# Cached attention, decode step: value tiles loaded through ScalarE's DMA queue

## The chip, the cores and the metric

One Trainium2 chip, one core of it. The metric is device microseconds of one execution. A core has TensorE (PE: matmuls, with PEld for the loads of their weights), VectorE (DVE), ScalarE (ACT), GpSimd (POOL) and SyncE (SP). Each engine works through its own list of instructions in order. DMAs are issued by instructions in such a list; here SyncE and ScalarE issue them, each into a queue of its own, and 16 DMA engines move the bytes of both.

## What is computed

A decode step for 4 sequences of one token: adaptive layer norm, attention over a cache of 4096 keys and values for each of 32 heads of 128, then a gated MLP. Cut to what matters:

```python
h = _layernorm(x) * (1 + ca) + sa                    # 4 x 512
q = (h @ wq).reshape(B, 1, 32, 128)
scores = einsum('bhqd,bhkd->bhqk', q, k_cache) * 128 ** -0.5
o = einsum('bhqk,bhkd->bhqd', softmax(scores), v_cache)
x = x + ga * (o.reshape(B, 1, 4096) @ wo)
h = _layernorm(x) * (1 + cb) + sb
x = x + gb * gated_mlp(h, w_in, w_sp, b_sp, w_out)
```

The keys and the values are 134 MB each, in bf16, and each is read once. All other inputs together are some 14 MB.

## The kernel before, in words

The 32 heads x 4 sequences are cut into 32 steps `i` of one sequence and four heads (`NT` = 32, `L` = 31 the last). A step has one K tile and one V tile, each 128 partitions x 128 rows x 128 (4 MB, 32 KB in each partition). There are two buffers of K tiles (named `kt`) and two of V tiles (`vt`); the last V tile uses a `kt` buffer. K2 and V2 stand for the tiles of step 2 in what follows.

The order of the work is written out by hand, in the loop at L533. For step `i` it holds, in this order:

- `mult(i, 0)` and `mult(i, 1)` (L291, VectorE): the two halves of the K tile are multiplied by the query, in place. They need K of step `i` to have landed.
- `reduce_d(i, 0)` and `reduce_d(i, 1)` (L297, TensorE): 16 matmuls with the identity that add up parts of each product; `sum8` (L306, VectorE) adds the rest.
- `scores(i-1)` (L311 to L332): the maximum on VectorE, then four Exps on ScalarE (L329) that write the weights `pbd`.
- `load_k(i + 2)` (L557): K of two steps on, into the buffer that step `i` frees; it waits for the last matmul of `reduce_d(i, 1)`.
- `pv(i-2)` (L369, TensorE): 32 matmuls of the weights with V of step `i-2`.
- `load_v(i)` (L570; `load_v(1)` at L568 in step 0): V of step `i`, into the buffer that `pv(i-2)` has just read.
- `o_pick(i-3)`, `o_cols`, `o_scale`, `project`: the output of an earlier step, picked out of PSUM and multiplied by `wo`.

So the loads go out as K0, K1, V0 ahead of the loop, then K2, V1 in step 0, K3 in step 1, K4 and V2 in step 2, and K and V in turn from there. All of them, and those of the weights, are issued by SyncE in this order. SyncE starts with `wq` (L92) and `wm` (L95). In step 2, behind V2, it loads `wo_sb` in four parts (L584) and `wo_last` (L589). ScalarE issues four small loads: `c_sb` and `x_sb` at the start (L86, L88) and two single numbers into `sp_t` in step 2 (L572, L573).

In step 30 come V30, then V31 in five pieces (32, 32, 32, 16 and 16 rows a partition, `TAIL`), the MLP's weights `win_sb` (L602, two parts) and `wout_sb` (L604), and the last part of `w_mod` (L608, into a `vt` buffer). Behind the loop runs the end of the kernel: `pv(30)`, the 128 matmuls of `o_last` with V31 (L396), the projection, the second layer norm, the MLP (L694, L719) and the output.

Each DMA counts up one of eight semaphores when it lands. They are dealt out in turn, so that a DMA may have to wait for an earlier one that used the same semaphore.

Of the kernel before, what the change touches and what calls it, by code (L numbers as in the profile page):

```python
# [16 lines left out]
KC = 64  # L17
RD = 8
TAIL = (32, 32, 32, 16, 16)
# [8 lines left out]
def kernel(  # L28
# [16 lines left out]
    nc = tc.nc  # L45
# [8 lines left out]
    NJ = SK * HQ // P  # L54
# [8 lines left out]
    L = NT - 1  # L63
# [33 lines left out]
    def kv_view(cache, i):  # L97
        g, b = divmod(i, B)
        v = cache[b, g * HQ:(g + 1) * HQ].rearrange("h s d -> (h s) d")
        return v.rearrange("(p n) d -> p n d", p=P)  # L100

    kts, vts = {}, {}

    def load(dst, src, cuts):
        n0 = 0
        for n in cuts:
            nc.sync.dma_start(out=dst[:, n0:n0 + n, :], in_=src[:, n0:n0 + n, :])
            n0 += n

    def load_k(i):  # L110
        if i < NT:
            kts[i] = kvp.tile([P, NJ, DH], BF16, name="kt", bufs=2)
            load(kts[i], kv_view(A_k_cache, i), (KC, NJ - KC) if i == L else (NJ,))

    def load_v(i):

        vts[i] = kvp.tile([P, NJ, DH], BF16, name="kt" if i == L else "vt", bufs=2)
        load(vts[i], kv_view(A_v_cache, i), TAIL if i == L else (NJ,))

    load_k(0)  # L120
    load_k(1)
    load_v(0)

    ident_bf = consts.tile([P, P], BF16, name="ident_bf")
# [21 lines left out]
        out=sel32, in_=ident_f.rearrange("p (q r) -> p r q", r=R), axis=AX.X, op=ALU.add  # L146
# [10 lines left out]
    for g in range(G):  # L157
        nc.vector.tensor_reduce(out=selg[:, g:g + 1], in_=idr[:, g], axis=AX.XY, op=ALU.add)
    nc.vector.tensor_reduce(
        out=sel4, in_=ident_f.rearrange("p (c b) -> p b c", b=B), axis=AX.X, op=ALU.add  # L160
# [3 lines left out]
        out=mask8, in_=ident_f.rearrange("p (h u) -> p h u", h=2 * HQ), axis=AX.X, op=ALU.add  # L164
# [42 lines left out]
    def normed(pool, src, name, then=None, last=None):  # L207
# [24 lines left out]
        out=sg, in0=cx, scalar1=-60.0, scalar2=-1.0, op0=ALU.max, op1=ALU.mult  # L232
# [6 lines left out]
    def mod_cols(s0, n, dst):  # L239
# [20 lines left out]
        out=hs, in0=modA[:, DJ:2 * DJ, :], scalar=1.0, in1=xn, op0=ALU.add, op1=ALU.mult  # L260
# [174 lines left out]
    for n in set(SETS):  # L435
        picks[n] = consts.tile([P, n, P], BF16, name=f"pick{n}")
        for a in range(n):
            u = P // n
            nc.vector.tensor_copy(
                out=picks[n][:, :, a * u:(a + 1) * u],  # L440
                in_=ident_bf.rearrange("p (u r) -> p r u", r=n),
# [91 lines left out]
    for i in range(NT):  # L533
# [21 lines left out]
        sum8(i, 0)  # L555
        reduce_d(i, 1)
        load_k(i + 2)  # L557
        if i >= 1:
            norm_a(i - 1)
# [7 lines left out]
        if i == 0:  # L567
            load_v(1)  # L568
        elif 2 <= i < L:
            load_v(i)  # L570
        if i == 2:
# [11 lines left out]
            for n in SETS:  # L583
                nc.sync.dma_start(  # L584
                    out=wo_sb[:, h0:h0 + n, :],
                    in_=A_wo[h0 * DH:(h0 + n) * DH].rearrange("(p r) n -> p r n", p=P),
# [48 lines left out]
    def sums():  # L635
# [20 lines left out]
        out=x1m, in0=x1[:, :, :, None].to_broadcast([P, DJ, B, HQ]),  # L656
# [5 lines left out]
        out=nv2, in0=mq2[:, 0:1], scalar=mq2[:, 0:1], in1=mq2[:, 1:2],  # L662
# [7 lines left out]
        out=hl, in0=xs, scalar=mq2[:, 0:1], in1=cbT[:, :, BL], op0=ALU.subtract, op1=ALU.mult  # L670
    )
    nc.vector.scalar_tensor_tensor(
        out=hT2[:, :, BL], in0=hl, scalar=rsl, in1=sbT[:, :, BL], op0=ALU.mult, op1=ALU.add
# [13 lines left out]
    def gate(h, part):  # L687
# [24 lines left out]
        out=zz.rearrange("p f g b -> p g b f"), in0=z1[:, None].to_broadcast([P, 2, B, NH]),  # L712
# [11 lines left out]
    for k in range(DJ):  # L724
# [7 lines left out]
        out=mq3, in_=ps3.rearrange("p (g b f) -> p g b f", g=2, b=B), axis=AX.X, op=ALU.add  # L732
# [4 lines left out]
        out=rs3, in0=mq3[:, 1], scalar=LN_EPS, in1=rs3, op0=ALU.add, op1=ALU.subtract  # L737
# [3 lines left out]
        out=g8[:, 0, :], in0=mq3[:, 0, :], scalar=-1.0, in1=g8[:, 1, :], op0=ALU.mult, op1=ALU.mult  # L741
# [5 lines left out]
        out=t3[:, 2], in0=yb[:, 0], scalar1=spf[:, 1:2], scalar2=None, op0=ALU.mult  # L747
    )
    nc.vector.tensor_tensor(
        out=g8, in0=g8, in1=rs3[:, None, :].to_broadcast([P, 2, B]), op=ALU.mult  # L750
    )
    nc.vector.tensor_tensor(
        out=t3[:, 0:2], in0=g8[:, :, :, None].to_broadcast([P, 2, B, DJ]), in1=yb, op=ALU.mult
# [3 lines left out]
        out=tt, in_=t3.rearrange("p g b j -> p b j g"), axis=AX.X, op=ALU.add  # L757
# [37 lines left out]
```

## Time and profile before

| | us |
|---|---|
| median of 3 runs | 667.61 (667.01 to 668.0) |
| the profiled execution | 667.16 |
| its span, first to last instruction | 665.4 |
| around the span | 1.76 |

| engine | busy us | share of the span | instructions |
|---|---|---|---|
| PE | 400.9 | 60% | 2674 |
| PEld | 175.3 | 26% | 2674 |
| DVE | 419.5 | 63% | 589 |
| ACT | 85.2 | 13% | 278 |
| POOL | 3.8 | 1% | 17 |

All traffic together is 283.15 MB at a mean of 426 GB/s. A K tile lands 23.0 us after its issue, a V tile 30.6 us (medians).

How to read what follows: times in a row of the trace count from the start of the span. A row of the order of time has start, duration, engine, line, operation, output and input, and in brackets the idle time of the engine ahead of it with what ended that. The rows of VectorE at L291 that end with a wait for a K tile show when that tile landed. A digit of the slices is the busy share of a fortieth of the span (16.6 us) in tenths. DMA share is the mean busy share of the 16 DMA engines; in short windows it can exceed 1. Rows marked SPq and ACTq are issues of DMAs by SyncE and ScalarE.

### The profile page before, as it was taken

How to read it: one execution, taken by the hardware profiler on the slowest of the kernel's cores; microseconds unless marked ns; L12 is line 12 of the kernel's file. 1: busy time of each engine (PE TensorE's matmuls, PEld its weight loads, DVE VectorE, ACT ScalarE, POOL GpSimd, SP SyncE). 2: the span in 40 equal slices, each digit the busy share in tenths (PEclk: the TensorE clock that was granted, in tenths of full speed). 3: DMA queues.
4: the chain of work that ended last, by engine and by line, in shares of the span. 5: the costliest groups of instructions: out<-in, count | busy, mean ns of one | idle time of the engine just before them, and what ended most of it. 6: DMA issues, size and time to landing. Idle time of an engine off the chain costs nothing.

```text
span 665.4 us, 6511 instructions
## 1 busy us (share of the span) xinstructions
PE 400.9 (60%) x2674; PEld 175.3 (26%) x2674; DVE 419.5 (63%) x589; ACT 85.2 (13%) x278; POOL 3.8 (1%) x17
## 2 busy tenths in 40 slices
PE   1195795556456647555665567566555467677676
PEld 0132331222122213222222223222222222232235
DVE  3485592776556776665577656657765666776833
ACT  1021120111011111101111110111110011111112
POOL 1000000000000000000000000000000000000000
PEclk9998987777898788889877778787767986887975
DMA  8999999999999999999999999999999999999996
GB/s 363 450 425 431 431 411 439 438 426 428 441 434 424 432 439 433 423 437 436 427 429 438 436 424 432 438 436 425 429 440 435 427 427 440 433 428 424 446 412 250
DMA packets 13537, 283.15 MB, mean 426 GB/s; under 512 B 1340, under 2 KB 3268, under 8 KB 4420
## 3 DMA queue, kind: packets, MB, share of 16 engines
q1 hardware_dynamic: 13488, 282.73, 99.0%
q8 instruction: 21, 0.34, 0.2%
q14 instruction: 8, 0.07, 0.0%
q10 hardware_dynamic: 20, 0.01, 0.0%
HBM read 282.73 MB, written 0.00 MB: 425 GB/s over the span
## 4 chain that ended last, share of the span: by engine, by line
DMA 57%; DVE 28%; PE 13%; issue 1%; SPq 0%; DVEq 0%
DMA kt<-in_A_k_cache_dram 51%; DVE kt L291 21%; PE red L297 12%; DMA vt<-in_A_v_cache_dram 3%; DMA wout_sb<-in_B_w_out_dram 3%; DVE osb L381 2%; DVE S L306 1%; DVE mrow L315 1%; DVE osb L377 1%; PE ops L369 1%; DVE mt L319 1%; DVE nM L321 0%; PE qps L277 0%; DVE mb L317 0%; DVE nM L322 0%
## 5 line engine op out<-in xcount | busy, mean ns | idle before, releaser
L297 PE MATMUL red<-kt,ident_bf 128*128 128x512 bf16 x1024 | 301.4, 460 | 235.0 <-DVE kt L291 235.0
L291 DVE TENSOR_TENSOR kt<-kt,qbc 128x8192 bf16<-128x8192 bf16 x64 | 282.8, 4420 | 185.3 <-DMA kt<-in_A_k_cache_dram 184.3
L297 PEld LDWEIGHTS <-ident_bf 128*128 128x128 bf16 x1024 | 118.5, 116 | 410.9 <-issue 283.8
L329 ACT ACTIVATE pbd<-S,nM 32x128 bf16<-32x128 f32 x128 | 74.0, 578 | 505.2 <-DVE nM L322 463.4
L369 PE MATMUL ops<-vt,pbd 128*16 128x512 bf16 x992 | 63.8, 393 | 1.3 <-DMA vt<-in_A_v_cache_dram 1.3
L306 DVE TENSOR_REDUCE S<-red 128x64 f32<-128x512 f32 x64 | 43.7, 684 | 5.9 <-PE red L297 5.9
L381 DVE SCALAR_TENSOR_TENSOR osb<-ops,selg,osb 128x128 f32<-128x128 f32 x93 | 32.6, 351 | 3.3
L329 ACT ACTIVATION_READ_ACCUMULATOR pbd<-S,nM 32x1 f32 x128 | 32.1, 251 | 0.0
L369 PEld LDWEIGHTS <-pbd 128*16 128x16 bf16 x992 | 23.4, 90 | 31.3 <-issue 9.5
L389 PEld LDWEIGHTS sm<-sel,osb 128*128 128x128 f32 x62 | 11.6, 194 | 8.0 <-issue 2.2
L377 DVE TENSOR_SCALAR osb<-ops,selg 128x128 f32<-128x128 f32 x31 | 10.1, 325 | 5.2 <-PE ops L369 5.2
L389 PE MATMUL sm<-sel,osb 128*128 128x4 f32 x62 | 9.3, 220 | 2.4 <-DVE osb L381 2.3
L281 ACT CAST qbc<-qps 128x512 bf16<-128x512 f32 x8 | 4.7, 587 | 45.4 <-PE qps L277 45.4
L277 PE MATMUL qps<-wq_sb,hTb 128*32 128x512 bf16 x128 | 9.2, 412 | 1.6 <-DVE hTb L265 0.9
L315 DVE TENSOR_REDUCE mrow<-S 128x1 f32<-128x128 f32 x32 | 9.2, 286 | 1.1
L245 PE MATMUL sm<-cT,wm_sb 128*128 128x4 bf16 x80 | 3.0, 173 | 8.2 <-DMA wm_sb<-in_w_mod_dram 8.2
L319 DVE STREAM_TRANSPOSE mt<-mb 128x32 f32<-128x32 f32 x32 | 6.8, 212 | 1.1
L340 DVE TENSOR_SCALAR rsb<-mask,rs 128x4 f32<-128x4 f32 x32 | 7.2, 224 | 0.4 <-ACT pbd L329 0.4
L321 DVE TENSOR_REDUCE nM<-mt 128x1 f32<-128x32 f32 x32 | 6.0, 186 | 1.1
L317 DVE COPY mb<-mrow 128x32 f32<-128x32 f32 x32 | 5.8, 181 | 1.1
L494 PE MATMUL sm<-wo_sb,od 128*4 128x512 bf16 x24 | 5.7, 379 | 0.0
L322 DVE TENSOR_SCALAR nM<-nM 128x1 f32<-128x1 f32 x32 | 4.9, 153 | 1.1
(136 smaller groups left out, 89.0 us busy)
## 6 DMA issues: line engine op xcount, KB each, us to landing
kt<-in_A_k_cache_dram SPq DMA_DIRECT2D x31, 4096.0 KB, 23.0
vt<-in_A_v_cache_dram SPq DMA_DIRECT2D x31, 4096.0 KB, 30.6
wq_sb<-in_A_wq_dram SPq DMA_DIRECT2D x1, 4096.0 KB, 12.2
kt<-in_A_k_cache_dram SPq DMA_DIRECT2D x2, 2048.0 KB, 16.5
wo_sb<-in_A_wo_dram SPq DMA_DIRECT2D x3, 1024.0 KB, 22.9
kt<-in_A_v_cache_dram SPq DMA_DIRECT2D x3, 1024.0 KB, 25.5
wm_sb<-in_w_mod_dram SPq DMA_DIRECT2D x1, 2560.0 KB
win_sb<-in_B_w_in_dram SPq DMA_DIRECT2D x2, 896.0 KB, 24.2
```

The lines of the kernel that those rows point to most:

```text
L277: nc.tensor.matmul(qp[R * q:R * (q + 1)], lhsT=hTb[:, k, b, :], rhs=wq_v[:, k, gs, q, :], start=(k == 0), stop=(k == DJ - 1), tile_positio ...
L291: nc.vector.tensor_tensor(out=kt, in0=kt, in1=bc(qbc[:, g, b, :], KC), op=ALU.mult)
L297: nc.tensor.matmul(red, lhsT=ident_bf, rhs=kt[:, :, m * RD:(m + 1) * RD], start=(m == 0), stop=(m == DH // RD - 1),)
L306: nc.vector.tensor_reduce(out=st[i, "S"][:, kc * KC:(kc + 1) * KC], in_=st.pop((i, "red", kc)), axis=AX.X, op=ALU.add,)
L315: nc.vector.tensor_reduce(out=mrow, in_=S, axis=AX.X, op=ALU.max)
L319: nc.vector.transpose(mt, mb)
L329: nc.scalar.activation(out=pbd[r, :, q], in_=S[r, :], func=AF.Exp, bias=nM[r, :], scale=att_scale, accum_out=rs[r, :],)
L340: nc.vector.tensor_scalar(out=st[g, "rsb"][:, b, :], in0=mask4, scalar1=st.pop((i, "rs")), scalar2=None, op0=ALU.mult)
L369: nc.tensor.matmul(opss[i % 2][g:g + G * HQ], lhsT=pbds[i % 3][:, n, :], rhs=vts[i][:, n, :], start=(m < 4), stop=(m >= NJ // G - 4), tile ...
L377: nc.vector.tensor_scalar(out=osb, in0=ops[:, 0, :], scalar1=selg[:, 0:1], scalar2=None, op0=ALU.mult)
L381: nc.vector.scalar_tensor_tensor(out=osb, in0=ops[:, g, :], scalar=selg[:, g:g + 1], in1=osb, op0=ALU.mult, op1=ALU.add,)
L389: nc.tensor.matmul(op, lhsT=st.pop((i, "osb")), rhs=sel4, start=True, stop=True)
```

## The change

V1 to V30 are issued by ScalarE into its own queue. V0 and V31, all K tiles and all weights stay with SyncE. The places of the calls in the loop stay where they are.

```diff
-    def load(dst, src, cuts):
+    def load(dst, src, cuts, eng):
         n0 = 0
         for n in cuts:
-            nc.sync.dma_start(out=dst[:, n0:n0 + n, :], in_=src[:, n0:n0 + n, :])
+            eng.dma_start(out=dst[:, n0:n0 + n, :], in_=src[:, n0:n0 + n, :])
             n0 += n
...
-            load(kts[i], kv_view(A_k_cache, i), (KC, NJ - KC) if i == L else (NJ,))
+            load(kts[i], kv_view(A_k_cache, i), (KC, NJ - KC) if i == L else (NJ,), nc.sync)
...
-        load(vts[i], kv_view(A_v_cache, i), TAIL if i == L else (NJ,))
+        load(vts[i], kv_view(A_v_cache, i), TAIL if i == L else (NJ,), nc.sync if i in (0, L) else nc.scalar)
```

In the order of instructions, ScalarE gets 30 DMA issues: V1 behind the third cast of the queries in step 0, V2 ahead of the two `sp_t` loads, and from there one V load between the four Exps of one step and those of the next. SyncE's list has the same DMAs without these 30. The lists of PE, DVE and POOL stay the same. The semaphores are dealt out anew: `wo_last` now shares one with V2 and waits for its landing (before, with `sp_t`); the first part of `win_sb` waits for V29, `wout_sb` for V31's first piece (before, for V30), and the first part of the last `w_mod` load for V30.

## The prediction

> **What bounds the kernel now.** I read the slices of the span first, then the table of windows, then the chain that ended last, then the order of time of single engines.
>
> From the page, the slices of DMA and the rate, the traffic by queue, and the chain:
>
> ```profile
> DMA  8999999999999999999999999999999999999996
> GB/s 363 450 425 431 431 411 439 438 426 428 441 434 424 432 439 433 423 437 436 427 429 438 436 424 432 438 436 425 429 440 435 427 427 440 433 428 424 446 412 250
> ...
> q1 hardware_dynamic: 13488, 282.73, 99.0%
> ...
> DMA 57%; DVE 28%; PE 13%; issue 1%; SPq 0%; DVEq 0%
> ```
>
> The 16 DMA engines are full from the first slice to the last but one, and one queue carries nearly all of it. The window from 20 to 640 us says it more sharply (its last two numbers are DMA share and GB/s):
>
> ```profile
> 20.00:640.00 620.00, 382.01 (x2327) 160.48 (x2324) 405.93 (x515) 77.68 (x260) 0.00 (x0) 0.83 1.00 432
> ```
>
> So this is a DMA-bound kernel without holes. A K or V tile is 128 x 16384 x 2 B = 4.19 MB. In the middle, K tiles land every 19.33 us (VectorE's multiplies begin at 293.30, 312.85, 332.17), with one V tile between: 8.39 MB per 19.33 us, 434 GB/s, 9.66 us a tile. That gives the price of any hole: each us in which no queue holds a transfer is a us on the end, since the DMAs have no slack later in which to make it up.
>
> **The change, step by step.** Thirty V loads (V1 to V30) leave SyncE's queue for ScalarE's. No byte, matmul or vector operation is added. The 30 issues move at 0.33 us each (the V rows of SyncE's issues). On ScalarE each now waits for pv(i-2), and behind it wait the four Exps of scores(i). In the middle V is issued 17.5 us after K(i) lands (312.85 to 330.36), while those Exps start some 25.7 us after it (312.85 to 338.51): 8 us of cover, cost 0. Without that cover the Exps would slip by as much as V's issue passes them.
>
> What does move the time is order. In one queue K2, V1, K3, K4, V2 land one after another, in the order in which the loop needs them. In two queues the heads share the 16 engines. Do they? ScalarE's queue has two small loads (sp_t) while SyncE's is full:
>
> ```profile
> 75.18 0.23 ACTq L572 DMA_DIRECT2D sp_t<-in_B_w_sp_dram  x1
> 75.45 0.27 ACTq L573 DMA_DIRECT2D sp_t<-in_B_b_sp_dram  x1
> ```
>
> K4 was issued earlier, at 74.18, and cannot land before 88.3 (K3 lands at 78.6, plus 9.66). Yet wo_last, which waits for sp_t, is issued at 80.86: sp_t's first half landed within 5.7 us (75.18 to 80.86), past K4's bytes. The queues take turns; I take equal shares, 19.3 us a tile while both are busy, and an overhead of 1.5 us into an empty queue (c_sb: issued 0.74, used 2.22).
>
> The Trainium skill, "DMA: Bandwidth & Descriptors", section "Queues, rings and completion order", says that each DMA engine goes round-robin between the queue rows it has work for, a packet at a time; the sp_t row agrees. Taken strictly by packets, V's long rows would beat the shorter rows of wo and of V31, and the sum by it would be that of the favoured V below, 682.
>
> *Step A, the first hole.* K0 lands at 28.88 and K2 at 59.29, three tiles later, so V0 lands near 49.6, V1 near 69, K3 at 78.6. After the change V1 is issued at 45.2 (behind the cast that ends there), K2 at 43.6 as before. Both then share the time from 49.6 to 69: K2 lands at 67.5 to 69, say 68.3, **9.0 us late**. Everything that refills the queues counts from K2:
>
> ```profile
> 59.29 4.43 DVE L291 TENSOR_TENSOR kt<-kt,qbc 128x8192 bf16<-128x8192 bf16 x1 [7.31 <-DMA kt<-in_A_k_cache_dram]
> ...
> 78.70 4.42 DVE L291 TENSOR_TENSOR kt<-kt,qbc 128x8192 bf16<-128x8192 bf16 x1
> ```
>
> K4 is issued 14.9 us after K2 lands (74.18), V2 17.6 after (76.89), wo 19.3 after (78.62). So K4 now goes out at 83.2. But K2, V1 and K3, all that is in the queues, are in by 78.6 as before. The DMAs are empty from 78.6 to 83.2 + 1.5 = 84.7: **+6.1 us**.
>
> *Step B, the second.* V2 goes out at 85.9 and iteration 3 starts at 68.3 + 19.4 = 87.7. K4 runs alone to 87.4 (1.2 MB), then beside V2: it lands at 101.2, V2, beside wo, at 106.7. K5 was issued 15.66 after its iteration began (78.70 to 94.36), which would be 103.4; but in the changed program wo_last waits for V2's landing (they share a semaphore), and K5 stands behind it: 106.7. The wo tiles with wo_last are another 4.19 MB, of which 1.2 are in; their rest runs beside V3 (issued 105.2) to 120.5. K5 follows, beside V3's rest and V4: lands 139.8 (V3 126.0, V4 145.3). K6, issued 15.66 after K4, is in by 152.2. K7 and V5 wait for K5: 139.8 + 15.66 + 1.5 = 157.0. Empty from 152.2 to 157.0: **+4.8 us**.
>
> After that K and V land side by side every 19.3 us, and each K is issued 15.7 us after the K two before it landed, 3.7 us ahead of need. Throttled matmuls take that to 18.8 (565.84 to 584.68), still ahead, and where one queue runs dry the other takes the rate: 0.
>
> *Step C, the end.* What decides there is V30, the last whole V tile, from which a serial chain runs to the output:
>
> ```profile
> 643.38 3.59 PE L369 MATMUL ops<-vt,pbd 128*16 128x512 bf16 x32 [1.31 <-DMA vt<-in_A_v_cache_dram]
> ...
> 661.10 0.61 PE L726 MATMUL sm<-cT,vt 128*128 128x4 bf16 x16
> ...
> 662.86 0.37 SPq L764 DMA_DIRECT2D out_dram<-xo  x1
> ```
>
> V30 lands at 643.4, 17.7 us ahead of the last weights (used at 661.1), which cover most of the 22.0 us of chain (643.4 to 665.4). In two queues, when K30 and V28 are in, SyncE's holds K31, V31, win, wout and w_mod's rest (11.66 MB), ScalarE's V29 and V30 (8.39 MB). At equal shares V30 lands together with V31, with 11.66 - 8.39 = 3.27 MB left, 7.5 us of the full rate; V28 trails K30 by up to 4 us, which makes it 5.5. I take 6.5: V30 comes 17.7 - 6.5 = 11.2 us later against the end of the DMAs. The chain behind it loses its four waits for DMAs (0.35 + 0.17 + 0.58 + 0.35 = 1.4 us), as those pieces now land first. **+9.8 us**.
>
> Sum: 6.1 + 4.8 + 9.8 = 20.7 us on the profiled execution's 667.16 (span 665.4 and 1.76 around it; 0.45 under the median, inside the runs' spread): **687.9, so 688 us**.
>
> **The rivals.** *Order of arrival, no change.* If the engines served both queues as issued, K2 would land at 59.3 and all stay as it is: 667. The 30 saved issues are worth nothing, as SyncE waits anyway. Against it: sp_t overtook K4.
>
> The Trainium skill, same page, section "Issuing engines are not separate DMA queues", says that issuing from several engines only saves the sequencer's issue time. By that alone the sum would be 0, 667 us; it speaks of bandwidth, not of which tile lands first, and no run here shows it yet.
>
> *One step only.* If SyncE's queue gets the larger share, K2 is early and A and B vanish, but V30 lands with the last byte: 661.1 + 20.6 + 1.8 = 683. If V is favoured, V30 is early and B grows: A 6.1 and B 9 give 682. With both partly mended, down to 676.
>
> *V takes two thirds or more.* Then each V lands long before its use, its two buffers are full, and K alone gates: a hole like B's in every second iteration, 4 to 5 us x 13: 740 or so. sp_t's 5.7 us do not speak for that, but do not exclude a milder form (700).
>
> *Faster.* Two queues keep the engines fuller: if the rate rose from 432 to the best late slice's 446, 3.2%, the 655 us of transfers would lose 20.6 us and just repay A to C; a gain needs more than that. Against it: the DMA share is 1.00 already.
>
> **How the numbers follow.** Forecast (A, B and C, 682 to 699) 0.65; one step only, 676 to 684, 0.17; over-served V, 700 and up, 0.08; no change 0.06; faster 0.04. Unknown sizes: A 5.2 to 6.7 (V1's start), B 2 to 9, C 7 to 14, noise in the matmul clock 3. Range: 676 to 702. Slower by over 0.2% (1.3 us, about what a measurement here can tell) 0.90, same 0.06, faster 0.04.
>
> **What would show it.** K2's first multiply near 68 instead of 59.3; two holes in the DMA rate before 160 us, then none; K and V landing side by side; pv(30) some 21 us ahead of the end, with no wait for V31 after it. A K2 at 59 breaks A and B; a V30 over 12 us ahead of the last transfer breaks C; holes after 200 us mean unequal shares.

## The result, and the profile after

The median goes from 667.4 us (667.01 to 668.0, six runs) to **694.43 us** (690.99 to 697.85, six runs): the ratio is 1.0407, with a 95% interval of 1.0386 to 1.0428. The forecast was 688, its range 676 to 702.

The profiled execution is the slowest of the six, 697.85 us with a span of 696.1. It is compared with the 667.16 us (span 665.4) of before, so it has to explain 30.7 us, 3.7 more than the medians differ. From the page of the changed kernel, the slices of DMA, the rate, the two queues and the chain:

```profile
DMA  8999599977999999999999999999999999999991
GB/s 367 447 421 446 219 433 416 443 338 286 432 426 440 426 427 431 432 422 434 429 435 435 427 433 435 421 424 428 433 432 433 431 431 428 422 406 426 433 405 38
...
q1 hardware_dynamic: 9168, 156.90, 53.2%
q10 hardware_dynamic: 4340, 125.84, 41.9%
...
DMA 59%; DVE 26%; PE 13%; issue 1%; ACT 0%; SPq 0%; DVEq 0%
DMA kt<-in_A_k_cache_dram 59%; DVE kt L291 19%; PE red L297 11%; DVE osb L381 2%; DVE S L306 1%; DVE mrow L315 1%; DVE mt L319 0%; DVE osb L377 0%; DVE nM L321 0%; DVE mb L317 0%; PE qps L396 0%; PE ops L369 0%; PE sm L195 0%; DVE nM L322 0%; ACT pbd L329 0%
```

The bytes are the same, now 126 MB of them in ScalarE's queue (q10). What is new are two dips: the fifth slice, 70 to 87 us, with 219 GB/s, and the ninth and tenth, 139 to 174 us. The last slice has 38 GB/s where it had 250. The table of windows of the changed kernel puts numbers to them (the last two of a row are DMA share and GB/s):

```profile
76.00:84.00 8.00, 8.00 (x58) 3.20 (x60) 3.90 (x3) 1.85 (x7) 0.00 (x0) 0.93 0.03 10
152.00:164.00 12.00, 10.08 (x63) 4.21 (x62) 7.02 (x12) 2.21 (x8) 0.00 (x0) 0.85 0.23 74
164.00:640.00 476.00, 284.13 (x1668) 120.40 (x1668) 314.81 (x395) 57.86 (x200) 0.00 (x0) 0.83 1.00 429
640.00:680.00 40.00, 24.82 (x209) 11.43 (x208) 20.41 (x40) 4.62 (x16) 0.00 (x0) 0.80 1.00 418
680.00:696.00 16.00, 10.68 (x256) 9.74 (x253) 6.40 (x33) 4.27 (x10) 1.08 (x5) 0.50 0.04 14
```

Against 434 GB/s the first hole is worth 8 x (1 - 10/434) = 7.8 us and the second 12 x (1 - 74/434) = 10.0 us. Between 164 and 640 us the rate is 429 GB/s where before had 432: another 476 x 3/432 = 3.3 us. The last weights land at 682.2 us and the span ends at 696.1, a tail of 13.9 us; before they landed at 661.4 with a tail of 4.0. So the last byte comes 20.8 us later, which the holes and the slower middle account for, and the tail is 9.9 us longer, which makes up the 30.7.

VectorE's multiplies in the order of time show which K tile was late. They are K2, K5 and the two halves of K31 in the changed kernel:

```profile
68.62 4.43 DVE L291 TENSOR_TENSOR kt<-kt,qbc 128x8192 bf16<-128x8192 bf16 x1 [17.36 <-DMA kt<-in_A_k_cache_dram]
...
145.59 4.42 DVE L291 TENSOR_TENSOR kt<-kt,qbc 128x8192 bf16<-128x8192 bf16 x1 [29.83 <-DMA kt<-in_A_k_cache_dram]
...
646.36 4.43 DVE L291 TENSOR_TENSOR kt<-kt,qbc 128x8192 bf16<-128x8192 bf16 x1 [3.34 <-DMA kt<-in_A_k_cache_dram]
...
660.84 4.42 DVE L291 TENSOR_TENSOR kt<-kt,qbc 128x8192 bf16<-128x8192 bf16 x1 [6.38 <-DMA kt<-in_A_k_cache_dram]
```

K2 lands at 68.62 and not at 59.29, and K5 at 145.59; VectorE stands still for 17 and 30 us before them. The end of the chain of waits of the changed kernel runs through K31's second half (2 MB, start and duration in us):

```profile
628.43 32.39 DMA kt<-in_A_k_cache_dram
660.84 4.43 DVE kt L291
665.32 6.44 PE red L297 x16
```

From its landing it is 35.3 us to the end of the span (660.84 to 696.1), through the reduction, pv(30), V31 and the MLP. The issue of V30 and the start of pv(30):

```profile
647.78 0.34 ACTq L107 DMA_DIRECT2D vt<-in_A_v_cache_dram  x1
...
676.74 2.54 PE L369 MATMUL ops<-vt,pbd 128*16 128x512 bf16 x32
```

No transfer is named ahead of pv(30). V30's load landed 17.6 us after its issue, at 665.4, 11 us before its use. So the tile that ends last is K31, not V30.

### The profile page after: what moved, and what is told of

Same layout as the page of the kernel before. It is cut to its first block, busy times and chain, and to the rows that moved or that the text cites. A ratio compares the mean times of both kernels' runs of the same rounds, so it can differ in the third digit from the quotient of the medians.

```text
span 696.1 us, 6515 instructions
## 1 busy us (share of the span) xinstructions
PE 394.6 (57%) x2674; PEld 174.2 (25%) x2674; DVE 419.7 (60%) x589; ACT 85.0 (12%) x278; POOL 3.8 (1%) x17
## 3 DMA queue, kind: packets, MB, share of 16 engines
q10 hardware_dynamic: 4340, 125.84, 41.9%
## 4 chain that ended last, share of the span: by engine, by line
DMA 59%; DVE 26%; PE 13%; issue 1%; ACT 0%; SPq 0%; DVEq 0%
DMA kt<-in_A_k_cache_dram 59%; DVE kt L291 19%; PE red L297 11%; DVE osb L381 2%; DVE S L306 1%; DVE mrow L315 1%; DVE mt L319 0%; DVE osb L377 0%; DVE nM L321 0%; DVE mb L317 0%; PE qps L396 0%; PE ops L369 0%; PE sm L195 0%; DVE nM L322 0%; ACT pbd L329 0%
## 5 line engine op out<-in xcount | busy, mean ns | idle before, releaser
L297 PE MATMUL red<-kt,ident_bf 128*128 128x512 bf16 x1024 | 296.7, 455 | 274.7 <-DVE kt L291 274.7
```

The source lines that it names most:

```text
L297: nc.tensor.matmul(red, lhsT=ident_bf, rhs=kt[:, :, m * RD:(m + 1) * RD], start=(m == 0), stop=(m == DH // RD - 1),)
```

## The experiments

Two theories of how queues share the 16 engines were set against each other. **E**, that of the prediction: equal shares of the bytes. **R**: the queues take turns row by row (a row is the stretch of one partition in one load), so that a queue's share goes by the length of its rows. K and V tiles have rows of 32 KB, K31's halves 16 KB, V31's pieces 8 and 4 KB, `wo_sb` 8 and 4 KB, `wo_last` 1 KB. R was formed from K31 above: its 4.19 MB took from 629.98, when K30 was in, to 660.84, or 31% of what 434 GB/s would have moved, about the third that a 16 KB row gets beside one of 32 KB. The trace also has the single packets of each queue: from 634 to 645 us SyncE's queue sent 97 of 16 KB and ScalarE's 99 of 32 KB, 1.6 MB against 3.2.

The kernel before ran beside each kernel on the same chip, with medians from 667.12 to 667.19 us. Unless another kernel is named, gains are against the 694.43 us of the changed one.

**e1: shorter V rows.** V0 to V30 in two loads of half a row each.

```diff
-        load(vts[i], kv_view(A_v_cache, i), TAIL if i == L else (NJ,), nc.sync if i in (0, L) else nc.scalar)
+        load(vts[i], kv_view(A_v_cache, i), TAIL if i == L else (KC, NJ - KC), nc.sync if i in (0, L) else nc.scalar)
```

> Edit: each of V1 to V30 is loaded as two DMAs of 64 rows a partition (16 KB instead of 32 KB), still in ScalarE's queue; V0 is cut as well. Theory R (the queues take turns row by row, so the share of a queue goes by the length of its rows): K with 32 KB rows gets two thirds while both are busy. K2's first multiply near 65 us instead of 68.62, the first hole 4 us instead of 8, K tiles ahead of V afterwards, time about 686 against 694. Theory E (equal shares by bytes): K2 at 68.6, both holes as they are, time 694. Either: no cost of the 30 further issues.

Measured: 686.78 us (ratio to before 1.0273 to 1.0307), 7.6 less. The row of K2's multiply and the queue of V in e1:

```profile
65.11 4.42 DVE L291 TENSOR_TENSOR kt<-kt,qbc 128x8192 bf16<-128x8192 bf16 x1 [13.40 <-DMA kt<-in_A_k_cache_dram]
```

```profile
q10 hardware_dynamic: 8660, 125.84, 43.0%
```

K2 lands where R put it, 65.11. The packets of ScalarE's queue follow the rows: 4340 became 8660, and 30 loads of 128 rows with 16 more packets each are 30 x (128 + 16) = 4320, twice that 8640 (the queue's small loads are the 20 left over). A row of 32 KB is one packet, and so is a row of 16 KB.

**e8: shorter still**, four loads with rows of 8 KB, `(32, 32, 32, 32)` in the same place.

> Edit: each of V0 to V30 as four DMAs of 32 rows a partition (8 KB), V1 to V30 in ScalarE's queue. Read for the start alone, as the end and the semaphores change too. Theory R: while both queues are busy, K has four fifths, so K2's first multiply comes near 62.5 us (68.6 with 32 KB rows, 65.1 with 16 KB rows, 59.3 without the change). Theory E: 68.6. If cutting V helps by something else (earlier starts of pv), K2 stays at 65.

Measured in a single run: 686.6 us. K2's multiply in e8:

```profile
63.49 4.43 DVE L291 TENSOR_TENSOR kt<-kt,qbc 128x8192 bf16<-128x8192 bf16 x1 [12.26 <-DMA kt<-in_A_k_cache_dram]
```

With V rows of 32, 16 and 8 KB K2 lands at 68.62, 65.11 and 63.49 (R had 62.5 for the last). The edits change the number of loads and the deal of the semaphores too, but the packets show the share itself: from 52 to 62 us SyncE's queue sent 69 packets and ScalarE's 64 in the changed kernel, 83 and 91 in e1, 110 and 106 in e8 (those of 4 bytes left out). The counts stay nearly equal while V's rows shrink, so that in e8 3.6 MB of K move beside 0.9 of V. E falls.

**e2: V1 back in SyncE's queue.**

```diff
-        load(vts[i], kv_view(A_v_cache, i), TAIL if i == L else (NJ,), nc.sync if i in (0, L) else nc.scalar)
+        load(vts[i], kv_view(A_v_cache, i), TAIL if i == L else (NJ,), nc.sync if i in (0, 1, L) else nc.scalar)
```

> Edit: V1 alone goes back into SyncE's queue. If V1 beside K2 makes the first hole (both theories): K2 at 59.3, no hole between 76 and 84 us, the second hole stays in some form (7 to 10 us near 145 us), time 687. If the holes come from the ScalarE queue itself (late issues, a slower queue), the first hole moves but stays, time 694.

Measured: 688.2 us (1.028 to 1.0344), 6.2 less. The windows of e2:

```profile
76.00:84.00 8.00, 3.37 (x70) 2.23 (x59) 5.34 (x4) 0.00 (x0) 0.00 (x0) 0.89 0.98 408
140.00:164.00 24.00, 16.61 (x78) 6.45 (x78) 18.56 (x31) 4.62 (x16) 0.00 (x0) 0.71 0.65 269
```

K2 lands at 59.12 and the first hole is gone; the second stays. So the first comes of V1 beside K2, and not of ScalarE's queue as such.

**e3: `wo_sb` and `wo_last` in ScalarE's queue too**, behind V2, so that their short rows no longer stand in front of K5.

```diff
-                nc.sync.dma_start(
+                nc.scalar.dma_start(
...
-            nc.sync.dma_start(out=wo_last, in_=A_wo[hl:H * DH].rearrange("(q p) n -> p q n", p=P))
+            nc.scalar.dma_start(out=wo_last, in_=A_wo[hl:H * DH].rearrange("(q p) n -> p q n", p=P))
```

> Edit: the four loads of wo_sb and that of wo_last are issued by ScalarE behind V2 instead of by SyncE. K5 then stands neither behind them nor behind V2's landing. Theory R: the first hole stays (8 us), K5 lands near 117 to 120 instead of 145.6, the second hole is gone, time 684. Theory E: K5 near 125, the second hole gone too, time 684 to 690. If the second hole comes from the V tiles alone, it stays near 10 us and the time at 694.

Measured: 686.92 us (1.0276 to 1.0307), 7.5 less. The windows of e3:

```profile
76.00:84.00 8.00, 8.00 (x42) 3.00 (x41) 4.30 (x3) 2.14 (x7) 0.00 (x0) 0.80 0.03 10
140.00:164.00 24.00, 11.74 (x59) 4.45 (x58) 12.46 (x19) 2.31 (x8) 0.00 (x0) 0.70 1.00 433
```

Now the second hole is gone and the first stays: K5 is there by 124.24, and its multiply waits for no transfer. The time is 3 us over R's 684. The two holes have separate causes. The move takes away both that `wo` stood in front of K5 and that `wo_last` waited for V2's landing in K5's queue. The trace of the changed kernel tells these apart. It has the issue of `wo_last`, and for the last part of `wo_sb` (issued at 89.05) and for `wo_last` the size and the us from issue to landing:

```profile
107.53 0.39 SPq L589 DMA_DIRECT2D wo_last<-in_A_wo_dram  x1
...
wo_sb<-in_A_wo_dram SPq DMA_DIRECT2D x1, 512.0 KB, 39.4
...
wo_last<-in_A_wo_dram SPq DMA_DIRECT2D x1, 512.0 KB, 28.4
```

So `wo_sb` was landing until 128.5 and `wo_last` until 135.9, and K5, issued behind them at 109.11, sent its first packet at 124. It stood behind their rows; the wait for V2, over by 107.5, held up its issue but not its transfer. Of the 512 rows of `wo_last` 46 started only after 129 us; why these lagged, no run here shows. From 108 to 120 us SyncE's queue sent 149 packets of 8 KB and ScalarE's 127 of 32 KB: 1.2 MB against 4.2.

**e4: both.** The edits of e2 and e3 together.

> Edit: both: V1 in SyncE's queue and wo_sb and wo_last in ScalarE's. Both theories: no hole ahead of 640 us, K5 as early as in the kernel before or earlier (108 to 118). What is left is the end: theory R has K31 (16 KB rows) behind V29 and V30 (32 KB rows), 676 to 678 us; theory E has V30 last, 680 to 682. If the end costs nothing, 667.

Measured: 677.92 us (1.0105 to 1.0186), 16.5 less. Neither hole is left (408 GB/s from 76 to 84 us, 433 from 140 to 164). The two alone bring 6.2 + 7.5 = 13.7, and the trace's two holes are 7.8 + 10.0 = 17.8 of an execution that took 3.4 us more than the median. The 16.5 lie between.

**e5: e4 with V29 and V30 back in SyncE's queue**, behind K31, where they were.

```diff
-        load(vts[i], kv_view(A_v_cache, i), TAIL if i == L else (NJ,), nc.sync if i in (0, 1, L) else nc.scalar)
+        load(vts[i], kv_view(A_v_cache, i), TAIL if i == L else (NJ,), nc.sync if i in (0, 1, L - 2, L - 1, L) else nc.scalar)
```

> Edit: the run with V1 in SyncE's queue and wo in ScalarE's (677.9 us), and V29 and V30 back in SyncE's queue as well, so that K31, V29, V30 and V31 land in the old order. If the end is what is left there: 667 to 669, no later than 1 us behind the kernel before. If a slower middle (two queues side by side for 500 us) is part of it: 672 or more.

Measured: 671.68 us (1.004 to 1.0081), 6.2 less than e4. The last half of K31 is multiplied at 634.96 with no wait for it; in e4 it came at 641.60. That is the whole step: from that multiply to the end of the span e4 has 35.2 us and e5 35.4. But 4.5 us over before remain, more than the forecast's "0" for the middle of the kernel.

**e6: the end alone.** V29 and V30 back in SyncE's queue, the two holes left in.

```diff
-        load(vts[i], kv_view(A_v_cache, i), TAIL if i == L else (NJ,), nc.sync if i in (0, L) else nc.scalar)
+        load(vts[i], kv_view(A_v_cache, i), TAIL if i == L else (NJ,), nc.sync if i in (0, L - 2, L - 1, L) else nc.scalar)
```

> Edit: the changed kernel with V29 and V30 alone back in SyncE's queue. Both holes ahead of 165 us stay (17 to 18 us). If the end is a part of its own, of 9 to 13 us: 682 to 685. If the end's loss only follows from the holes: 694.

Measured: 691.34 us (1.0341 to 1.0374), only 3.1 less, a miss. The profiled executions differ by 697.85 - 691.71 = 6.1, as K31's last half comes at 654.66 instead of 660.84; but the changed kernel's typical run is faster than its profiled one. So the end is worth some 3 to 6 us. Whether it is worth less beside the holes than without them, no run here settles: the two medians differ by no more than the spread of the executions allows.

**e7: K31 in one load**, with 32 KB rows, in e4.

```diff
-            load(kts[i], kv_view(A_k_cache, i), (KC, NJ - KC) if i == L else (NJ,), nc.sync)
+            load(kts[i], kv_view(A_k_cache, i), (NJ,), nc.sync)
```

> Edit: the run with V1 in SyncE's queue and wo in ScalarE's (677.9 us), with K31 loaded as one DMA with 32 KB rows instead of two with 16 KB rows. Theory R (turns by rows): K31's share goes from a third to a half; the multiply of its second half starts near 632 to 634 us instead of 641.6, time 672 to 676. Theory E (shares by bytes): K31 lands as before, its first half is waited for longer, 678 to 681.

Measured: 676.52 us (1.0132 to 1.0165), 1.4 less than e4, which is within the spread of e4's executions (672.99 to 679.58), and just over R's 672 to 676. The issue of K31 and the multiplies of its two halves, in e4 and then in e7:

```profile
614.86 2.72 SPq L107 DMA_DIRECT2D kt<-in_A_k_cache_dram  x2
...
641.60 4.42 DVE L291 TENSOR_TENSOR kt<-kt,qbc 128x8192 bf16<-128x8192 bf16 x1 [2.07 <-DMA kt<-in_A_k_cache_dram]
```

```profile
610.78 0.33 SPq L107 DMA_DIRECT2D kt<-in_A_k_cache_dram  x1
...
632.78 4.43 DVE L291 TENSOR_TENSOR kt<-kt,qbc 128x8192 bf16<-128x8192 bf16 x1 [9.91 <-DMA kt<-in_A_k_cache_dram]
640.78 4.41 DVE L291 TENSOR_TENSOR kt<-kt,qbc 128x8192 bf16<-128x8192 bf16 x1
```

The tile does land sooner after its issue, 22.0 us instead of 26.7 (from 614.86 in e4). But the first multiply can now begin only when all is in, and the second half follows at 640.78 instead of 641.60. The transfer goes as R has it; the second multiply, forecast for 632 to 634, and the time hardly follow, since the halves gave an overlap that is lost.

**e9: why the middle is slower.** e5 with V0 to V30 in two loads of 16 KB rows, as in e1 (the expectation names V2 to V28, those in ScalarE's queue).

> As e5 (V1, wo, wo_last, V29 and V30 placed so that neither the two holes nor the late end remain), and V2 to V28 cut into two loads of half rows (16 KB). It is to tell why the middle of e5 still moves 428 GB/s from 200 to 580 us where the kernel before moves 433. Theory M1, the reissue comes late: K's queue runs out before the next K is issued, because K lands in 19 us beside an equal V. With V's share down to a third, K lands some 5 us earlier against its need; then the rate from 200 to 580 us rises to 431 or more, and the time falls to 667.5 to 670, unless waits for V come up. Theory M2, two queues of large loads move less, whoever is first: 428 GB/s and 671 to 674 again.

Measured: **668.26 us** (1.0006 to 1.0024). From 200 to 580 us, before, then e5, then e9:

```profile
200.00:580.00 380.00, 230.34 (x1332) 95.67 (x1332) 251.88 (x319) 46.38 (x160) 0.00 (x0) 0.82 1.00 433
```

```profile
200.00:580.00 380.00, 224.60 (x1310) 93.47 (x1311) 245.62 (x304) 43.95 (x152) 0.00 (x0) 0.82 1.00 428
```

```profile
200.00:580.00 380.00, 225.57 (x1343) 94.62 (x1342) 248.92 (x309) 45.54 (x158) 0.00 (x0) 0.82 1.00 431
```

Two queues as such hardly cost time: with V in half rows it is within 0.15% of before, 3.4 us less than in e5. A K tile lands 19.5 us after its issue in e9 and 23.2 in e5 (medians). Time and rate are those that M1 forecast, but its mechanism isn't what the packets show. Counted by queue over these 380 us, K's queue is empty for 15 us in e5, while V's moves 427 GB/s, and for 89 us in e9, at 429. With V's queue empty, for 26 us, e5 moves 416, which is worth 1 us (26 x 16/432). For the rest both queues hold packets in e5, and the rate is 428 (before, counted in the same way: 432). So most of the loss isn't where a queue runs dry. Nor is it shown that whole V tiles are the reason (M2), for e7, whose loads in this stretch are those of e5, has:

```profile
200.00:580.00 380.00, 224.74 (x1317) 93.94 (x1318) 247.83 (x310) 43.95 (x152) 0.00 (x0) 0.82 1.00 431
```

The same loads move 428 GB/s in the one and 431, the rate of e9, in the other. The cause of the 3.4 us stays open.

**e10: is it the start, or any place where the second queue begins?** Only V10 to V28 go to ScalarE.

```diff
-        load(vts[i], kv_view(A_v_cache, i), TAIL if i == L else (NJ,), nc.sync if i in (0, L) else nc.scalar)
+        load(vts[i], kv_view(A_v_cache, i), TAIL if i == L else (NJ,), nc.scalar if 10 <= i <= 28 else nc.sync)
```

> Only V10 to V28 go through ScalarE's queue; V0 to V9, V29 to V31, wo and all else stay in SyncE's. The start and the end are then those of the kernel before. Theory R with one hole at each change from one queue to two: V10 shares with the K tile in front of it, that K lands some 9 us late once, as K2 did, and the DMAs are empty once for 4 to 8 us near 230 to 290 us; then 672 to 680 us. If the holes come from the start of the kernel alone (cold queues, wo), there is none in the middle and the time is 668 to 672 us (only a slower middle).

Measured: 675.91 us (1.012 to 1.0173), 8.8 over before. The multiply of K12 (issued at 231.18, 2.0 us ahead of V10 in the other queue) and the windows of e10:

```profile
269.99 4.42 DVE L291 TENSOR_TENSOR kt<-kt,qbc 128x8192 bf16<-128x8192 bf16 x1 [21.55 <-DMA kt<-in_A_k_cache_dram]
```

```profile
280.00:290.00 10.00, 8.45 (x65) 4.06 (x64) 9.79 (x14) 0.44 (x2) 0.00 (x0) 0.99 0.40 139
320.00:580.00 260.00, 152.60 (x906) 63.95 (x905) 165.19 (x206) 30.08 (x104) 0.00 (x0) 0.82 1.00 430
```

K12 takes 38.8 us, K14 goes out late (286.24), and from 282 to 287 the engines stand empty: 10 x (1 - 139/434) = 6.8 us. With 260 x 3/433 = 1.8 us of slower middle that is 8.6 of the 8.8. So a hole comes at 280 us as at 80, at the place where the second queue begins.

From these runs the 27.0 us between the medians come to: 16.5 for the two holes (e4), 6.2 for the end (e4 to e5), 3.4 for the middle (e5 to e9), and 0.9 left over (e9 to before). By the intervals the first two are good to some 3 us each, the third to 2.

## Why the prediction was right, and where it was off

The sign was right, and so was the mechanism of the two holes: the change reorders landings, and what that costs is DMA time with nothing in the queues. The rule for the shares, equal bytes, was not: the queues take turns by rows. The time was 6 us short, and it came that near in part by luck, as B and the middle were put too low and C too high.

- **Step A held.** K2 at 68.62 against 68.3, K4 issued at 83.25 against 83.2, and e2 shows that V1 alone does it. Equal shares came out because K2 and V1 both have rows of 32 KB. V1 went out at 43.90, as the cast ahead of it began, and not at 45.2, which mattered little. The hole's size, 7.8 us in the trace against 6.1, was a little small: it opened at 77 and not at 78.6. e2 gives 6.2.
- **Step B had the right place and half the size.** It said K5 at 139.8 and 4.8 us. It was 145.59 and 10.0 us. The term that was mis-sized is the time of `wo` beside V3, "their rest runs beside V3 (issued 105.2) to 120.5", at equal shares: `wo_last` landed at 135.9. Rows of 8 KB beside rows of 32 KB moved 1.2 MB against 4.2, and K5 stood behind them; that it then came 9.7 us after `wo_last`, and not 19.3, gave some of it back. e3, with `wo` out of K5's way, removes the hole and brings 7.5 us. The rival "V favoured" had this with 9 us.
- **The middle was not 0** but about 3.4 us (e5 to e9). The reason given, "where one queue runs dry the other takes the rate", held when K's queue was the empty one: 427 GB/s in e5 and 429 in e9. What had no term is a lower rate while both queues hold packets, 428 in e5 against 432 before; its cause is open. The 19.33 us between K tiles is one of two gaps, 19.55 and 19.32; their mean, 19.44, gives 432 GB/s and not 434, which moves no term by more than some 0.1 us.
- **Step C named the wrong tile.** It forecast +9.8 us from V30. V30 landed at 665.4, 16.8 us ahead of the last weights at 682.2, and the prediction's own sign against C was a V30 over 12 us ahead of the last transfer. K31 ended last: it lay in 16 KB rows against V29 and V30 with 32 KB. That the trace's tail is 9.9 us longer is next to the 9.8 by luck, and the medians make the end 3.1 to 6.2 us.
- **The rivals.** No change (667) fell with K2. "V favoured" was right for V beside short rows and had a fitting B, 9, and with it 682; it was short because it made the end cheap, seeing V30 and not K31. Its A was 6.1, near the 6.2 of e2. V so far ahead that K alone gates in every second iteration (740) didn't come: from 200 us on there is no hole, K and V having rows of one length there. Faster would have needed a rate over 446 GB/s all along; two slices reach it, with 447 and 446.

The packet rule that the prediction weighed, from the Trainium skill's "DMA: Bandwidth & Descriptors", section "Queues, rings and completion order", is the one that e1 and e8 bear out, with a whole row as the packet: 68.62, 65.11 and 63.49 us. The other, from its section "Issuing engines are not separate DMA queues", that issuing from several engines only saves issue time, is not enough here: the bytes and nearly the rate stayed, and the time rose by 27 us, as the tile that the loop needs next lands later.

## What to carry to other kernels

Here one queue kept the DMA engines full, at 432 GB/s, and a second one added no rate and took away the order. In such a case ask which tile is needed next, what now lands beside it, and whether the issues that hang on it leave the queues empty. In these runs a queue's share went by the length of its rows (1.6 MB of 16 KB rows beside 3.2 of 32 KB), so that pieces cut small for overlap (K31) and weights with short rows (`wo`) lost against whole tiles in the other queue. If two queues must be used, begin the second with something that no early tile competes with, keep short rows in the queue nobody waits behind, and cut the less urgent stream finer; e9, with all of these, took 668.26 us.

## What was not expected of the hardware

A row is one packet, up to 32 KB (e1), and the two queues take turns by such packets: 97 of 16 KB beside 99 of 32 KB from 634 to 645 us of the changed kernel, 110 of 32 KB beside 106 of 8 KB from 52 to 62 us of e8.

Executions also differ more with two queues, though not always. The six runs of the changed kernel spread over 6.9 us (690.99 to 697.85) and the four of e4 over 6.6, those of before over 1.0 and the eleven of e9 over 0.5 (667.99 to 668.46). e9 has more slack for K, but e3, which still has the first hole, spreads over 0.5 too, so that the slack isn't shown to be the reason.
